# Holding back the loads of q and k of units 6 and 7 behind GpSimd memsets, in an attention and squared-ReLU MLP kernel

## The chip, the cores and the metric

One core of a Trainium2 chip. The metric is device time in microseconds (us) of one execution of the whole program. A "profile" is one execution recorded by the hardware profiler; its span is about 1.8 us shorter than the device time (393.8 against 395.61 us in the kernel before). "Fast" runs are those less than 1.5% above the fastest run of the same kernel; the others carry the label "slow". Engine names in the profile: PE is TensorE (PEld its weight loads), DVE VectorE, ACT ScalarE, POOL GpSimd, SP SyncE; an engine name with a q, such as SPq, is that engine's sequencer, which issues DMAs. L345 is line 345 of the kernel. The granted clock is the share of full speed that TensorE's clock had, 1.00 or 0.50 at any one moment here.

## The reference

```python
# q, k, v: (8, 12, 448, 64) fp32;  w_in: (768, 2048);  w_out: (2048, 768)
scores = q @ k^T / 8
attn   = max(scores, 0)**2 / 448
x      = (attn @ v), heads merged           # (3584, 768)
out    = max(x @ w_in, 0)**2 @ w_out        # (3584, 768) fp32
```

The 96 heads are handled in 24 units of four heads, three units for each of eight batches.

## The kernel before

The kernel is written through its own list scheduler. Every operation is added with a cost; the scheduler simulates five engines, decides an order for each, and then emits the instructions in that order. **The scheduler's times decide only the order.** In the trace a load that the plan starts "not before 50 us" is not held until 50 us by anything: the two planned so here go at 6.18 and 6.66 us (below), just behind the casts that free their buffers (5.03 to 6.16 us).

The load of q or k of a unit into one of four fp32 buffers (`raw`) already has a `gate`, which the kernel before never uses:

```python
    def load_qk(n, w, after=0.0, gate=False):
        b, u = divmod(n, NU)
        buf = Buf("raw")
        ...
        deps = []
        if gate:
            deps.append(plan.add(
                [("POOL", 0.1, 0.1, lambda: nc.gpsimd.memset(buf.tile[0:1, 0, 0:1], 0.0))],
                bufs=[buf], after=after))
        eng, name = (nc.scalar, "ACT") if (n, w) == (0, "q") else (nc.sync, "SP")
        op = plan.add([(name, 0.5, 0.5, lambda: eng.dma_start(out=tile_of(), in_=src), QK)],
                      deps, [buf], after=after)
        return op, buf, tile_of
```

The memset writes one element of the buffer. The load overwrites it, so the program makes the load wait for it: a way to tie a DMA to a place in GpSimd's order.

The start of the kernel, in the order of GpSimd's DMA queue (all of these convert fp32 to fp16 on the way: a load of q or k lands as 224.0 KB on the page, one in fp32 as 448.0 KB):

```python
    for w in "kq":
        raws[0, w] = load_qk(0, w)              # unit 0: SyncE and ScalarE queues, fp32
    ...
    for w in "kq":
        casts[1, w] = load_early(1, w, 1.4, 1.0)   # GpSimd queue
    load_v(0, 1.4, 1.1)
    for w in "kq":
        casts[2, w] = load_early(2, w, 1.4, 1.2)
    load_v(1, 1.4, 1.3)
    load_v(2, 1.4, 1.4)
    w1_ops = [load_w1(0, 1.4, 1.5)]                # w_in, four tiles of 1.6 MB
    w1_ops += [load_w1(i, 8.0, 1.6) for i in range(1, 4)]
    ...                                            # units 3 to 5 and w_out later, same queue
```

Units 6 and up are loaded in fp32 by SyncE, cast on GpSimd (`blk<-raw`, L372) and turned by DMA transposes (`qkt<-blk`, L408). TensorE turns q and k of units 0 to 5 itself (L392). Dummy "filler" matmuls (L932) keep it busy where the plan sees idle time in the first 45 us. L453 are the scores, L518 attn times v, L580 and L629 the product with w_in, L729 and L794 that with w_out.

## Time and profile before

| | |
|---|---|
| median of 3 runs | 393.39 us (391.31 to 393.70) |
| profiled run | 395.61 us, span 393.8 us |
| TensorE busy | 382.4 us (97%) |
| mean granted clock of the profiled run | 0.981 |

First the page of the profile: its first line, and the granted clock in 40 equal slices of the span (about 9.8 us each, in tenths; 9 is 90% or more).

```profile
span 393.8 us, 8375 instructions
...
PEclk9859999999999999999999999999999999999999
```

The third slice has a 5: TensorE ran at about half clock around 20 to 30 us. Next the chain of waits (start, length, what), the work that ended last followed back from the end:

```profile
4.94 10.46 DMA g<-in_q_dram
...
20.40 0.33 PE mm L932
...
26.24 0.41 PE sp L453 x4
...
27.19 2.56 PE mm L629 x6
...
47.17 3.37 PE mm L580 x24
...
70.66 7.97 DMA qkt<-blk
```

In this profile one load, q of unit 2, holds the chain for 10.5 us of the start. The timeline of TensorE (start, length, what, and in brackets the idle time before it and what ended it) shows the gap that it leaves:

```profile
12.23 0.42 PE L518 MATMUL mm<-comb,vs 64*64 64x128 f16 x16
15.44 0.30 PE L392 MATMUL mm<-ident,g 128*64 128x128 f16 x4 [2.79 <-DMA g<-in_q_dram]
```

The timeline of SyncE up to 54 us shows what else was loading:

```profile
0.74 5.82 SPq L345 DMA_DIRECT2D raw<-in_k_dram  x2
6.66 0.42 SPq L345 DMA_DIRECT2D raw<-in_q_dram  x1
52.31 0.37 SPq L345 DMA_DIRECT2D raw<-in_k_dram  x1
53.75 0.37 SPq L345 DMA_DIRECT2D raw<-in_q_dram  x1
```

Two k loads are merged in the first line: unit 0 at 0.74 and unit 6 at 6.18. So both loads of unit 6, 0.92 MB, go out at 6 us, far ahead of their use near 67 us. Those of unit 7 go at 52.31 and 53.75 us, as their buffers hold unit 5 until then: TensorE reads it there until 52.28 and 53.71. GpSimd's timeline has the same late load from another side, since its issue of the last w_in tile had to wait for it; and it has the first casts of unit 6:

```profile
15.68 0.82 POOL L427 DMA_DIRECT2D w<-in_moe_w_in_dram  x1 [3.12 <-DMA g<-in_q_dram]
...
67.22 3.41 POOL L372 CAST blk<-raw 128x896 f16<-128x896 f32 x3
```

Last, busy time by windows of 3.41 us, cut at the moments at which the granted clock changed (the recorded stretches of one clock, but for the last, are 10.24, 13.65 and 361.81 us long in this trace: 3, 4, 106 times 3.41 us; columns: window, its length, PE busy and count, PEld, DVE, ACT, POOL, granted clock, DMA share, GB/s):

```profile
10.07:13.48 3.41, 2.27 (x66) 1.38 (x64) 1.85 (x2) 3.39 (x5) 1.94 (x3) 1.00 1.17 289
13.48:16.89 3.41, 1.45 (x46) 1.03 (x47) 1.05 (x3) 0.68 (x1) 1.19 (x2) 1.00 1.20 230
16.89:20.31 3.42, 3.33 (x53) 1.54 (x48) 2.02 (x4) 3.29 (x4) 2.53 (x4) 0.50 1.24 206
...
27.13:30.54 3.41, 3.41 (x23) 1.22 (x25) 0.72 (x2) 1.41 (x4) 0.00 (x0) 0.50 1.24 207
```

The window with the gap has TensorE busy for 1.45 of 3.41 us; right at its end the clock halves, and it stays at half for four such windows, 13.65 us.

### The profile page before, as it was taken

To read this page: it belongs to the slowest core of one execution; us is meant where nothing else is said; L and a number is where in the kernel's file an instruction comes from. 1 tells how busy PE (TensorE), PEld (TensorE's weight loads), DVE (VectorE), ACT (ScalarE), POOL (GpSimd) and SP (SyncE) were. 2 spreads that over 40 slices of the span, in tenths; PEclk is the share of its full clock that TensorE was granted. 3 is DMA by queue.
4 is the path that set the end of the run, shared out by engine and by line. 5 is a ranking of instruction groups with operands and counts; after the bars stand their busy time and mean duration, and the time that the engine had idled before them with its cause. 6 is when DMAs were issued, how large, how long until landed. Compare 5 with 4: busy or idle time off the path is not lost.

```text
span 393.8 us, 8375 instructions
## 1 busy us (share of the span) xinstructions
PE 382.4 (97%) x3324; PEld 201.6 (51%) x3324; DVE 269.0 (68%) x390; ACT 279.0 (71%) x414; POOL 166.4 (42%) x163
## 2 busy tenths in 40 slices
PE   8699999899999999999999999999999999999995
PEld 4435556454455445544555545544455545555553
DVE  3456878877796687657888665866886767256841
ACT  4758989799867887778977687885886876244111
POOL 7544835477473464354744733522701531001000
PEclk9859999999999999999999999999999999999999
DMA  9999996999837976497177677477383001210243
GB/s 194 244 207 168 147 231 113 195 220 204 165 67 122 240 183 97 134 213 125 54 147 183 158 183 165 84 162 163 60 118 80 2 2 37 65 40 2 50 96 96
DMA packets 69672, 51.34 MB, mean 130 GB/s; under 512 B 36865, under 2 KB 69633, under 8 KB 69633
## 3 DMA queue, kind: packets, MB, share of 16 engines
q1 hardware_dynamic: 52112, 35.86, 37.9%
q0 software_dynamic: 16928, 14.09, 24.5%
q10 hardware_dynamic: 592, 0.85, 0.6%
q8 instruction: 26, 0.43, 0.5%
q14 instruction: 14, 0.11, 0.1%
HBM read 45.61 MB, written 11.01 MB: 144 GB/s over the span
## 4 chain that ended last, share of the span: by engine, by line
PE 89%; DMA 5%; DVE 2%; ACT 2%; POOL 1%; issue 1%; POOLq 0%; DVEq 0%
PE mm L580 37%; PE mm L794 29%; PE sp L453 10%; PE mm L518 8%; DMA g<-in_q_dram 3%; DMA qkt<-blk 2%; PE mm L932 2%; PE mm L629 1%; DVE comb L773 1%; PE mm L729 1%; PE mm L392 1%; POOL g L362 1%; ACT at L487 1%; DVE rel L480 0%; ACT rel L483 0%
## 5 line engine op out<-in xcount | busy, mean ns | idle before, releaser
L580 PE MATMUL mm<-xt,w 128*128 128x448 f16 (+1 forms) x768 | 149.2, 346 | 0.0
L489 POOL TENSOR_TENSOR at<-rel 128x896 f16<-128x896 f32 (+1 forms) x45 | 73.0, 1623 | 115.4 <-ACT rel L483 87.6
L487 ACT ACTIVATE at<-rel 128x896 f16<-128x896 f32 (+1 forms) x123 | 111.9, 932 | 7.1 <-DVE rel L480 4.1
L564 DVE SCALAR_TENSOR_TENSOR g<-mm,g 128x448 f16<-128x448 f32 (+1 forms) x128 | 76.7, 605 | 52.0 <-ACT g L569 51.5
L580 PEld LDWEIGHTS <-w 128*128 128x128 f16 x768 | 72.1, 98 | 70.4 <-issue 12.1
L480 DVE TENSOR_SCALAR rel<-sp 128x896 f32<-128x896 f32 (+2 forms) x87 | 90.1, 1040 | 22.9 <-PE sp L453 21.3
L569 ACT ACTIVATE g<-mm 128x448 f16<-128x448 f32 (+1 forms) x128 | 67.8, 535 | 41.3 <-PE mm L580 40.8
L483 ACT ACTIVATE rel<-sp 128x896 f32<-128x896 f32 (+2 forms) x87 | 78.3, 908 | 9.1 <-PE sp L453 8.4
L794 PEld LDWEIGHTS <-comb 128*128 128x128 f16 x416 | 39.7, 98 | 30.0 <-issue 3.8
L453 PE MATMUL sp<-qkt,qkt 64*64 64x448 f16 (+2 forms) x756 | 52.6, 347 | 2.3 <-DMA qkt<-blk 1.9
L713 ACT ACTIVATE part<-mm 128x384 f32<-128x384 f32 x40 | 19.6, 490 | 40.4 <-PE mm L794 38.8
L372 POOL CAST blk<-raw 128x896 f16<-128x896 f32 x36 | 37.0, 1037 | 24.2 <-issue 12.1
L806 DVE SCALAR_TENSOR_TENSOR part<-mm,part 128x384 f32<-128x384 f32 x52 | 28.6, 554 | 23.6 <-ACT part L713 13.3
L794 PE MATMUL mm<-wt,comb 128*128 128x384 f16 x208 | 36.8, 326 | 0.2 <-DVE comb L773 0.2
L794 PE MATMUL mm<-w,comb 128*128 128x384 f16 x208 | 36.8, 326 | 0.1
L518 PE MATMUL mm<-at,vs 64*64 64x448 f16 (+1 forms) x672 | 35.5, 344 | 0.0
L794 PEld LDWEIGHTS <-g 128*128 128x128 f16 x264 | 25.1, 98 | 19.3 <-issue 3.1
L453 PEld LDWEIGHTS <-qkt 64*64 64x64 f16 x756 | 18.0, 107 | 29.8 <-issue 26.0
L695 POOL COPY rest<-g 128x1024 f16<-128x1024 f16 x8 | 9.8, 1226 | 49.8 <-DVE g L564 49.8
L794 PE MATMUL mm<-w,g 128*128 128x384 f16 x176 | 30.8, 326 | 0.0
L422 POOL DMA_DIRECT2D vs<-in_v_dram x48 | 29.7, 627 | 2.1 <-DMA g<-in_k_dram 0.9
L518 PEld LDWEIGHTS <-vs 64*64 64x64 f16 x756 | 22.7, 111 | 12.5 <-issue 2.9
(60 smaller groups left out, 225.1 us busy)
## 6 DMA issues: line engine op xcount, KB each, us to landing
out_dram<-part SPq DMA_DIRECT2D x108, 96.0 KB, 2.2
raw<-in_k_dram SPq DMA_DIRECT2D x19, 448.0 KB, 3.9
raw<-in_q_dram SPq DMA_DIRECT2D x18, 448.0 KB, 4.5
vs<-in_v_dram POOLq DMA_DIRECT2D x48, 112.0 KB, 4.0
w<-in_moe_w_in_dram POOLq DMA_DIRECT2D x4, 768.0 KB, 16.6
w<-in_moe_w_out_dram POOLq DMA_DIRECT2D x4, 768.0 KB, 13.0
g<-in_k_dram POOLq DMA_DIRECT2D x4, 224.0 KB, 11.5
g<-in_q_dram POOLq DMA_DIRECT2D x4, 224.0 KB, 11.7
```

The source lines that it names most:

```text
L372: return lambda: fn(blk.tile.rearrange("p t (f d) -> p f t d", f=2), tile_of().rearrange("p f (t d) -> p f t d", d=D))
L422: nc.gpsimd.dma_start(out=buf.tile[64 * r:64 * r + 64], in_=src[:, u, hs])
L453: nc.tensor.matmul(sp[64 * c:64 * c + 64, e, c0:c0 + w].rearrange("p (t c) -> p t c", c=TP), lhsT=kT[r, t, 64 * e:64 * e + 64], rhs=qT[r, ...
L480: dve(n, lambda: nc.vector.tensor_scalar(out=rel(), in0=sp.tile[:, :, 0:width], scalar1=0.0, scalar2=SK, op0=ALU.max, op1=ALU.mult)),
L483: act(n, lambda: nc.scalar.activation(out=rel(), in_=sp.tile[:, :, 0:width], func=AF.Relu, scale=SK))],
L487: act(n, lambda: nc.scalar.activation(out=dst(), in_=rel(), func=AF.Square)),
L489: lambda: nc.gpsimd.tensor_mul(dst(), rel(), rel()))],
L518: nc.tensor.matmul(banks[f].tile[64 * e:64 * e + 64, c0:c0 + w], lhsT=vs[r, e ^ c, t * D:(t + 1) * D], rhs=a[r, e, :], start=(t == 0), sto ...
L564: nc.vector.scalar_tensor_tensor(out=dst, in0=src, scalar=0.0, in1=dst, op0=ALU.is_gt, op1=ALU.mult)
L569: nc.scalar.activation(out=dst, in_=src, func=AF.Square)
L580: nc.tensor.matmul(bank.tile[:, c0:c0 + w], lhsT=w1[f // 4][:, m, f % 4 * P:(f % 4 + 1) * P], rhs=xts[b].tile[:, m, cols], start=(m == 0), ...
L794: nc.tensor.matmul(buf.tile[:, 0:HALF], lhsT=lhs()[:, j, :], rhs=w[:, j, :], start=(first and j == 0), stop=(j == NH - 1), skip_group_chec ...
```

## The change

The intent: stop the loads of units 6 and 7 from competing with the start, by using the gate for these two units. The memset is planned at 50 us, so it sits in GpSimd's order after the operations planned before that.

```diff
-                        raws[n, w] = load_qk(n, w, max(50.0, coming(n) - 26.0))
+                        raws[n, w] = load_qk(n, w, max(50.0, coming(n) - 26.0), n < 8)
```

As the scheduler sees the memsets, its order changes too, though not at once: TensorE's order is the same for the first 40% of its instructions.

## The prediction

> **What bounds the kernel now.** TensorE: busy 382.4 of 393.8 us on the page; 89% of the chain of waits. Its direct waits sum to under 7 us (view of waits), so most of what can be won is in the start. There the chain goes through one DMA: the load of q of unit 2, issued at 4.94 us, lands at 15.4, and TensorE idles 2.8 us for it (12.65 to 15.44, timeline). Then the granted clock falls: 1.00 up to 16, 0.50 until about 30 (windows of 2 us). [...]TensorE is recorded busy throughout, so some 6.9 us are lost.
>
> **Why that load is late.** The scheduler's plan starts the loads of unit 6 at 50 us, but the hardware waits only for their buffers, free since the casts of unit 0: issued at 6.1 and 6.7 us (timeline of SyncE). Their 0.92 MB move from about 10 to 15.4 us, while the GpSimd queue (unit 2, v, w_in) moves only 0.66 of some 1.2 MB: 2.6 us lost.[...]
>
> **What the change does.** Four memsets of one element (about 0.1 us each; GpSimd is 42% busy: nothing) stand in GpSimd's order after its third 128x896 square, which ends at 59.6 us before. Loads of unit 6 move from 6 us to behind that; those of unit 7 (52.3 and 53.8 before, against w_out) too. TensorE's order is unchanged over its first 40%; later a few squares and blocks swap: taken as 0 +-1.5 us.
>
> **Gain, at the start.**
> - q of unit 2 lands 2.6 us earlier; TensorE's gap shrinks to under 0.5 us: -2.5 us.
> - Without the gap the clock should stay at 1.0 (chance 75-80%): -6.9 us at most.
> - Not all is kept. Each w_in tile lands about 2.7 us earlier (estimated 19.3, 23.4, 26.6, 30.2), and a full-speed TensorE reaches the second 1.3 us too early. ScalarE must do 17.4 us of work (14 to 40 us) in about 20, and is the chain already at 37 to 43. I give back 3 us.
> Net: about -6.5 us by the mark that was 43 us; everything after it shifts along, bound by TensorE.
>
> **Cost, at 53 to 65 us.** Four loads, 1.84 MB, at some 300 GB/s (seen at 2 to 4 us): 6 to 7 us. The casts began at 67.2 us, 7.6 us after the third square, and DMA was nearly idle from 64 to 68: casts wait under 1 us. The 1.9 us wait for transposes at 77 us stays, shifted.
>
> **Predicted: 387.0 us; 382.5 to 391.5 holds it 8 times in 10.** Faster by over 2%: 0.28; within 2%: 0.70; slower: 0.02.
>
> **What would show it.** Right: no wait of TensorE over 1 us at 11 to 15 us; granted clock 1.0 from 6 to 40; no SyncE load between 7 and 50 us, then four in a row; the first L580 matmul at about 41 us, not 47.1; later stages shifted equally. Wrong: a half-clock stretch anyway (only 2 to 3 us won); TensorE idle before the L629 matmuls, or ScalarE saturated from 20 to 40; casts waiting for DMA at 60 us and a longer transpose wait.
>
> **What would make it wrong.** [...]the throttle's cause isn't the gap; or the later reordering costs or saves over 1.5 us.

2.5 + 6.9 - 3 = 6.4 us, put at about 6.5, and 6.5 below 393.5 is 387.0. The 6.9 us of the clock is the estimate: half of the 13.65 us that the profile before shows at half clock, and that the gap brings the half clock was at this point an inference from one profile, in which the one follows the other. The memsets' 0.1 us was an estimate as well; they were recorded at 88 ns each.

## The result, and the profile after

| | before | changed |
|---|---|---|
| median, runs of this comparison | 393.52 us (391.31 to 393.70, 4 runs) | 387.19 us (387.09 to 387.20, 4 runs) |
| ratio of fast runs | | 0.9851, 95% interval 0.9816 to 0.9886 |
| span of the profiled run | 393.8 us | 385.4 us |
| mean granted clock there | 0.981 | 0.998 |

Ratios in this text are the mean time of one kernel's fast runs over that of the other's of the same rounds, so not quite the ratio of the medians. The change is faster by 1.5%, within 2%.

The page: the 8 and the 5 in the clock row are gone.

```profile
span 385.4 us, 8379 instructions
...
PEclk9999999999999999999999999999999999999999
```

The chain of waits, the lines that answer to those above:

```profile
16.25 0.26 PE sp L453 x4
...
17.55 0.21 PE mm L932
...
20.72 1.29 PE mm L629 x6
...
39.03 3.37 PE mm L580 x24
...
62.53 7.83 DMA qkt<-blk
```

The same six L629 matmuls take 1.29 us in place of 2.56, and the first L580 group starts at 39.03, 8.14 us earlier. TensorE's timeline at the same place:

```profile
11.46 0.42 PE L518 MATMUL mm<-comb,vs 64*64 64x128 f16 x16
11.81 0.30 PE L392 MATMUL mm<-ident,g 128*64 128x128 f16 x4
...
13.99 0.36 PE L518 MATMUL mm<-comb,vs 64*64 64x128 f16 x11
15.16 0.27 PE L518 MATMUL mm<-comb,vs 64*64 64x128 f16 x5 [0.80 <-issue]
```

The turning of q of unit 2 goes at 11.81 without a wait; a smaller gap of 0.80 us appears three us later. The profile names no cause for it ("issue"), but these matmuls read v of unit 2, whose load lands at 14.9 us in this trace. SyncE now issues nothing after unit 0 until 51.5 us (the first line again merges two loads), then four loads in a row:

```profile
0.75 51.14 SPq L345 DMA_DIRECT2D raw<-in_k_dram  x2
52.00 0.41 SPq L345 DMA_DIRECT2D raw<-in_q_dram  x1
52.51 0.41 SPq L345 DMA_DIRECT2D raw<-in_k_dram  x1
53.02 0.42 SPq L345 DMA_DIRECT2D raw<-in_q_dram  x1
```

GpSimd: q of unit 2 has landed by 11.94 in place of 15.68; a w_in tile that releases an issue at 22.90 is the second one; the memsets cost 0.19 us; the casts start without waiting for a load.

```profile
11.94 0.82 POOL L427 DMA_DIRECT2D w<-in_moe_w_in_dram  x1 [0.30 <-DMA g<-in_q_dram]
...
22.90 0.76 POOL L362 DMA_DIRECT2D g<-in_q_dram  x1 [2.38 <-DMA w<-in_moe_w_in_dram]
...
51.40 0.19 POOL L342 MEMSET raw<- 1x1 f32 x4
...
59.09 3.41 POOL L372 CAST blk<-raw 128x896 f16<-128x896 f32 x3
```

The windows, 3.41 us long as before and counted back from the one change of clock in that run, at 383.80 us, and then all that TensorE waited for (view of waits: total us, times, longest):

```profile
8.33:11.75 3.42, 3.42 (x88) 2.38 (x88) 2.37 (x5) 3.41 (x4) 3.07 (x4) 1.00 1.26 202
11.75:15.16 3.41, 2.52 (x92) 1.64 (x80) 3.03 (x5) 3.41 (x5) 3.21 (x4) 1.00 1.26 205
15.16:18.57 3.41, 3.41 (x66) 1.77 (x65) 2.37 (x4) 3.13 (x5) 2.17 (x5) 1.00 1.21 190
```

```profile
PE sp L453 <- DMA qkt<-blk: 1.8, 1, 1.8
PE mm L929 <- DVE part L926: 1.2, 1, 1.2
PE mm L518 <- issue: 0.8, 1, 0.8
```

The emptiest of these windows has 2.52 of 3.41 us, and the clock stays up. What is left is 1.8 us near 70 us, for the DMA transposes of unit 6.

### The profile page after: what moved, and what is told of

It is laid out like the page before. It is cut to its first block, busy times and chain, and to the rows that moved or that the text cites. A ratio compares the mean times of both kernels' runs of the same rounds, so it can differ in the third digit from the quotient of the medians.

```text
span 385.4 us, 8379 instructions
## 1 busy us (share of the span) xinstructions
PE 376.1 (98%) x3324; PEld 200.0 (52%) x3324; DVE 266.2 (69%) x387; ACT 277.1 (72%) x413; POOL 173.1 (45%) x171
## 4 chain that ended last, share of the span: by engine, by line
PE 90%; DMA 4%; DVE 3%; ACT 2%; issue 1%; POOL 0%; POOLq 0%; DVEq 0%
PE mm L580 37%; PE mm L794 29%; PE sp L453 10%; PE mm L518 8%; DMA qkt<-blk 2%; PE mm L932 2%; DMA g<-in_q_dram 2%; DVE comb L773 1%; PE mm L629 1%; PE mm L729 1%; DVE rel L480 1%; PE mm L392 1%; ACT at L487 1%; ACT rel L483 0%; DVE part L806 0%
## 5 line engine op out<-in xcount | busy, mean ns | idle before, releaser
L580 PE MATMUL mm<-xt,w 128*128 128x448 f16 (+1 forms) x768 | 149.0, 346 | 0.0
L489 POOL TENSOR_TENSOR at<-rel 128x896 f16<-128x896 f32 (+1 forms) x49 | 79.9, 1630 | 105.0 <-ACT rel L483 81.0
L487 ACT ACTIVATE at<-rel 128x896 f16<-128x896 f32 (+1 forms) x119 | 108.2, 931 | 3.2 <-PE mm L518 2.3
L580 PEld LDWEIGHTS <-w 128*128 128x128 f16 x768 | 72.1, 98 | 70.6 <-issue 12.3
L480 DVE TENSOR_SCALAR rel<-sp 128x896 f32<-128x896 f32 (+2 forms) x86 | 89.0, 1039 | 18.4 <-PE sp L453 16.6
L483 ACT ACTIVATE rel<-sp 128x896 f32<-128x896 f32 (+2 forms) x88 | 79.2, 908 | 8.0 <-PE sp L453 7.2
L453 PE MATMUL sp<-qkt,qkt 64*64 64x448 f16 (+2 forms) x756 | 51.0, 338 | 2.1 <-DMA qkt<-blk 1.8
L453 PEld LDWEIGHTS <-qkt 64*64 64x64 f16 x756 | 17.7, 105 | 28.0 <-issue 23.8
L518 PEld LDWEIGHTS <-vs 64*64 64x64 f16 x756 | 22.0, 107 | 12.7 <-issue 3.0
## 6 DMA issues: line engine op xcount, KB each, us to landing
g<-in_k_dram POOLq DMA_DIRECT2D x4, 224.0 KB, 11.3
```

Of the source, the lines that this page charges most:

```text
L453: nc.tensor.matmul(sp[64 * c:64 * c + 64, e, c0:c0 + w].rearrange("p (t c) -> p t c", c=TP), lhsT=kT[r, t, 64 * e:64 * e + 64], rhs=qT[r, ...
L480: dve(n, lambda: nc.vector.tensor_scalar(out=rel(), in0=sp.tile[:, :, 0:width], scalar1=0.0, scalar2=SK, op0=ALU.max, op1=ALU.mult)),
L483: act(n, lambda: nc.scalar.activation(out=rel(), in_=sp.tile[:, :, 0:width], func=AF.Relu, scale=SK))],
L487: act(n, lambda: nc.scalar.activation(out=dst(), in_=rel(), func=AF.Square)),
L489: lambda: nc.gpsimd.tensor_mul(dst(), rel(), rel()))],
L518: nc.tensor.matmul(banks[f].tile[64 * e:64 * e + 64, c0:c0 + w], lhsT=vs[r, e ^ c, t * D:(t + 1) * D], rhs=a[r, e, :], start=(t == 0), sto ...
```

## The experiments

The theory: (a) the early loads of unit 6 delay q of unit 2 in the DMA engines; (b) TensorE's gap halves its clock; (c) the half clock is the larger part of the cost. Rivals: the clock falls for another reason; contention of unit 7 with w_out matters; the scheduler's reordering made the gain. Twelve experiments were run, all with correct results. "Clock" below is each run's mean granted clock.

| run | median us (range), runs | clock of the runs | ratio to before in the same rounds |
|---|---|---|---|
| before_again | 392.18 (388.53 to 394.55), 6 | 0.980 to 0.999 | 0.998 (0.991 to 1.005) |
| order_kept | 388.40 (387.82 to 389.69), 6 | 0.993 to 1.0 | 0.991 (0.986 to 0.996) |
| only_unit7 | 391.31 (389.01 to 394.01), 6 | 0.981 to 1.0 | 0.998 (0.992 to 1.004) |
| fill_gap | 389.33 (388.20 to 389.58), 6 | 0.997 to 1.0 | 0.992 (0.987 to 0.997) |
| after_again | 387.70 (387.29 to 389.00), 6 | 0.994 to 1.0 | 0.986 (0.983 to 0.989) |
| gap_back | 392.29 (390.98 to 394.13), 6 | 0.987 to 0.993 | 0.997 (0.994 to 1.001) |
| gap_back_filled | 390.28 (388.96 to 392.36), 6 | 0.996 to 1.0 | 0.992 (0.989 to 0.996) |
| k6_early | 388.14 (387.06 to 389.89), 6 | 0.993 to 1.0 | 0.987 (0.984 to 0.990) |
| gate8 | 385.90 (385.21 to 386.67), 6 | 0.997 to 1.0 | 0.984 (0.980 to 0.988) |
| hold8_14 | 385.85 (385.44 to 389.93), 6 | 0.987 to 1.0 | 0.986 (0.981 to 0.990) |
| after_third | 388.56 (387.15 to 390.10), 6 | 0.993 to 1.0 | 0.990 (0.985 to 0.995) |
| gate8_again | 385.67 (385.35 to 389.26), 6 | 0.990 to 1.0 | 0.983 (0.979 to 0.988) |

The four groups of runs were the first four, the next four, the next two and the last two; each was on another chip.

### before_again: how much the time before hangs on the clock

No edit.

> The kernel before, unchanged, to see its spread run by run with the granted clock of each run. Theory (the time of the kernel before hangs on how many windows of half clock follow the gap): single times differ by steps of about 2 us (391.3, 393.5, 395.6 were seen) and go with the mean granted clock, about 1.7 us of time for each 0.0043 of clock[...]. Rival (the spread is something else, such as DMA): times and clocks unrelated.

Measured: the same program took from 388.5 to 394.6 us in this run, and its clock went from 0.999 to 0.980. With the runs of before there are 48 fast runs (two more, 394.55 and 395.11 us at clock 0.983, are left out; with them the slope below is 281). A straight line through them is 389.3 us + 276 us x (1 - clock), with a correlation of 0.94. Four runs at a clock of at least 0.998 took 389.3 us in the mean; nine at 0.981 or less, 394.4.

It follows that the kernel before is not a 393 us kernel with noise but a 389.3 us kernel that loses 0 to 5 us to half clock, run by run; in the mean 276 x (1 - 0.9882) = 3.3 us. The profiled run, at 395.61 us, was the worst. The expected 1.7 us for each 0.0043 of clock, an estimate that takes half of the time at half clock as lost, came out as 1.2. The estimate would hold if all of TensorE's work took twice as long: the slope would then be the span, 393 us. It is 70% of that. The chains above fit this: the dense L629 group takes 2.56 against 1.29 us, twice as long, but L453 x4 takes 0.41 against 0.26 and L932 0.33 against 0.21, 1.6 times.

Two cautions about the clock figures. The record falls to 0.50 once more at the very end, after TensorE's last matmul (in the changed kernel from 383.80 us on, with TensorE busy for 0.00 us after that), and this alone makes its 0.998. In none of the eight kept profiles at 0.998 to 1.0 was the clock at half during TensorE's work, so amounts worked out from a mean clock are some 0.3 us too large. And each record begins only at 4 to 7 us (6.65 in the first profile, 4.92 in that of the changed kernel); before that the views print 1.00 for want of a record.

The profile of this run (394.55 us) also shows that the first one was unusual. Here q of unit 2 landed at 13.2 us and not at 15.4, and TensorE waited for two loads in turn, q and then v of unit 2. The chain goes through v (first line; then two lines of the view of waits):

```profile
6.32 10.43 DMA vs<-in_v_dram
...
PE mm L392 <- DMA g<-in_q_dram: 1.6, 2, 1.2
PE mm L518 <- DMA vs<-in_v_dram: 1.0, 1, 1.0
```

It is the same in only_unit7 (1.3 and 1.0 us), and in fill_gap too q lands at 13.0 and the chain goes through v. So in three of the four profiles with both loads of unit 6 early, the wait is shared between q and v. Why q was 2 us later in the first profile is not known.

### order_kept: the gain without the reordering

```diff
-        op = plan.add([(name, 0.5, 0.5, lambda: eng.dma_start(out=tile_of(), in_=src), QK)],
+        op = plan.add([(name, 0.5, 0.5, lambda: (n in (6, 7) and nc.gpsimd.memset(tile_of()[0:1, 0, 0:1], 0.0), eng.dma_start(out=tile_of(), in_=src)), QK)],
```

> The kernel before with the same four memsets, emitted together with the loads so that the scheduler does not see them: the order of TensorE, VectorE, ScalarE and SyncE stays as before, only the memsets are added on GpSimd. Theory (all of the gain is the start, the reordering after 40% of TensorE's work is worth nothing): 387 us within 1 us, clock 1.0 throughout, ratio to before about 0.984. Rival (a good part of the gain came from the reordering): over 389 us.

Measured: 388.4 us; ratio 0.991. This is 1.4 us over the expected value, between the theory and its rival, and two of the six runs were at clocks of 0.993 and 0.994, which the theory excluded. The four clean runs took 388.1 us in the mean; those of the changed kernel took 387.4 (below), but on other chips. Its first L580 group starts at 39.03 us as in the changed kernel, so the start is fully there. The profile puts the difference at one place: TensorE waits 2.7 us near 70 us for the transposes of unit 6, against 1.8, and the scores after that wait start 0.93 us later than in the changed kernel (71.42 and 70.49). At the end the two are 1.03 us apart (last VectorE step of the chain at 382.16 and 381.13). So in these two profiles the reordering over the last 310 us is worth about 0.1 us. The edit itself explains the rest only in part: its memsets for unit 7 come one GpSimd operation later, so those loads are issued at 53.75 and 54.23 us in place of 52.51 and 53.02. That this is what makes the transposes later was not tested.

### only_unit7: is the contention with w_out worth anything?

```diff
+        ... the same line, with the memset only for n == 7
```

> The same, but only the two loads of unit 7 are held back; those of unit 6 go at 6 us as before. Theory (only the loads in the start matter): as before, 393.5 us within 1 us, q of unit 2 lands at 15.4, half clock from about 16. Rival (the contention with w_out at 52 to 64 us matters too): faster by 1 us or more, with the start unchanged.

Measured: ratio 0.998, interval 0.992 to 1.004: the same as before. Its median of 391.3 lies 2 us under that of before, which was to be within 1 us, but the clock explains this: its two runs at clock 1.0 took 389.0 and 389.7 us, just what the line of before gives there. The mean of the six, 391.5, is also what the line gives at their mean clock of 0.991 (391.7). So no effect of unit 7 alone was seen. Two expectations missed: q of unit 2 landed at 13.3 us and not at 15.4, and the half clock began at 18.12 us, after the window with the wait for v. In the change unit 7 cannot be seen apart: its loads come after those of unit 6 in SyncE's order anyway.

### fill_gap: early loads as before, but no idle TensorE

Twelve dummy 128x512 matmuls are put into TensorE's order just before the transposes of q of unit 2, in the kernel before; everything else stays.

```diff
-            for t in ts:
+            for t in ["fill"] * 12 * ((n, w, ts[0]) == (2, "q", 0)) + list(ts):
```

The cut leaves out the second changed line, which makes each "fill" a 128x512 matmul of the idle tile into the same PSUM bank. The twelve took 2.76 us in the profile.

> The kernel before, all loads as before, with 12 dummy matmuls (128x512, some 2.6 us) on TensorE just before it waits for q of unit 2. Theory (the idle gap is what halves the clock): the load still lands at about 15.4, but the clock stays at 1.0, and TensorE reaches its first L580 matmul some 4 to 6 us earlier than before; total 388 to 390. Rival 1 (the clock falls for another reason, such as the thin 64x64 matmuls after 16 us): half clock as before and 393 to 394 us. Rival 2 (DMA bound the start anyway, so the clock cost nothing): clock 1.0 but no gain, TensorE idle before the L629 matmuls.

Measured: 389.33 us, clock 0.997 or more in all six runs, range 1.4 us in place of 6. The windows of its profile show the place of the gap filled, and the clock up:

```profile
13.35:16.76 3.41, 3.14 (x72) 1.76 (x70) 1.86 (x4) 1.09 (x3) 2.56 (x3) 1.00 1.21 233
16.76:20.17 3.41, 3.41 (x61) 1.70 (x61) 2.68 (x4) 3.41 (x5) 2.52 (x5) 1.00 1.25 209
```

The first L580 group starts at 41.19 us. So (b) holds: the loads were as before and only TensorE's idle time was filled, and the half clock was gone. One expectation missed: q of unit 2 landed at 13.0 us and not at 15.4, so the dummies, which lasted to 14.5, outlasted the wait for it. The value, 389.3, is also the end of the line above at clock 1. What remains to the changed kernel is about 2 us: TensorE turns q of unit 2 at 14.51 us, after the dummies, in place of 11.81.

### gap_back and gap_back_filled: held loads, with the gap put back

In the changed kernel, one added matmul at the same place reads v of unit 2, whose load lands later, so TensorE idles with no added DMA. The second kernel puts 15 dummies ahead of it (3.41 us in its profile).

```diff
-            for t in ts:
+            for t in ["wait"] * ((n, w, ts[0]) == (2, "q", 0)) + list(ts):
```

Cut as before: the second changed line makes "wait" a matmul that reads v of unit 2. The second kernel has 15 "fill" ahead of it.

> The changed kernel with one added matmul on TensorE just before it turns q of unit 2, which reads v of unit 2 and so waits for that load (it lands at about 14 to 15 us; TensorE is there at 11.8). All loads stay held back, so the gap is back without the DMA contention. Theory (the gap halves the clock): half clock from about 16 us in most runs; time 389 us plus up to 6, spread by several us from run to run, going with the clock. Rival (the contention, not the gap, cost the time): clock 1.0 and 389 to 390 us at most.

> The same added wait for v of unit 2, with 15 dummy matmuls of 128x512 (some 3.2 us) ahead of it, so that TensorE is as late as in the run with the gap, but not idle. Theory: clock 1.0, spread under 1 us, 389.5 us within 1 us. Rival (the delay itself costs, not the clock): same time and same clock as with the gap.

Measured: with the gap 392.29 us, and the clock at 0.987 to 0.993 in every run; filled 390.28 us and a clock of 0.996 or more. TensorE idles 3.63 us in the profile of the first, and its windows show the clock fall at the end of the empty one, with all loads of units 6 and 7 still held:

```profile
10.72:14.13 3.41, 0.85 (x29) 0.47 (x23) 1.10 (x2) 2.74 (x3) 3.07 (x4) 1.00 1.25 203
14.13:17.55 3.42, 2.35 (x35) 1.32 (x39) 1.17 (x3) 0.01 (x1) 1.02 (x2) 0.50 1.18 189
```

The filled kernel turns q of unit 2 as late (15.89 us) as the one with the gap (15.72). In the latter's profile one of the three windows at half clock lies near 75 us (75.57 to 78.99), after a wait of 2.3 us for the transposes of unit 6, so the gap in the start answers for two thirds of the clock that was lost there.

Together with fill_gap this is a two by two: early or held loads, idle or filled gap. The clock follows the idleness in both rows and not the loads. The filled one spread over 3.4 us, more than the 1 us expected; one run of 392.36 us at clock 0.996 stays unexplained.

### k6_early: half of the early bytes

The edit of order_kept, with the memset for q of unit 6 and for unit 7, but not for k of unit 6.

> The kernel before in its own order, memsets hidden from the scheduler, with q of unit 6 and both loads of unit 7 held back but k of unit 6 let go at 6 us: half of the early bytes (0.46 MB). Theory (bytes ahead of q of unit 2 set the gap): q of unit 2 lands about 1.3 us later than with all held, a gap of about 1 us; clock mostly 1.0, about 389 us, a run or two slower. Rival (any load there is enough): as before, 392 to 394 us with the clock down in most runs.

Measured: 388.14 us, about as fast as with all held (388.40). TensorE waits 1.08 us for q of unit 2, and its window keeps the clock:

```profile
10.75:14.16 3.41, 2.33 (x77) 1.62 (x74) 2.08 (x4) 2.77 (x3) 1.91 (x3) 1.00 1.21 244
```

So (a) holds: q of unit 2 lands at 11.3 to 12.1 us in the nine profiles with no early load, at 12.7 with 0.46 MB, and with 0.92 MB at 13.0 to 13.3 in three profiles and at 15.4 in the first. In the profile of k6_early the clock was at half for one window after the wait for the transposes near 70 us (72.19 to 75.60). The clock can fall there too, and did in before_again (76.36 to 79.77) and gap_back; so a part of the clock lost by before is lost there and not in the start.

### after_again and after_third: is the changed kernel immune?

No edit.

> The changed kernel once more, for its spread with the granted clock of each run (only four runs of it are known, 387.1 to 387.2). Theory (its start has no gap long enough to halve the clock[...]): all runs within 0.5 us of 387.2, clock 0.997 or above. Rival[...]: one run in four or so at 389 to 391 us with a clock near 0.990.

> The changed kernel, on the same chip and in the same rounds as the version that holds the loads of unit 8 too, as the two had been timed on different chips. Theory (the wait near 70 us costs it 1.8 us, and now and then one window of half clock after it): 387.3 us, one or two runs of six 1.3 to 1.7 us slower at a clock near 0.994.

Measured: the theory of the first, that all runs are at clock 0.997 or more, fails. Of the 16 runs of the changed kernel, twelve have such a clock and took 387.4 us in the mean; four took 389.0 to 390.1 us with clocks of 0.993 to 0.996. The first four runs had been lucky. The second expected one or two slow runs of six, 1.3 to 1.7 us slower; three came, 2.1 to 2.7 us above the clean ones. No profiles were kept of the four, so it is not shown whether the clock fell in the start or near 70 us.

### gate8 and hold8_14: the wait near 70 us

In the changed kernel the loads of unit 8 are issued at 60.04 and 61.95 us, between the transposes of unit 6 (60.51 and 62.53). Two ways to move them:

```diff
 gate8, from the changed kernel
-   load_qk(n, w, max(50.0, coming(n) - 26.0), n < 8)
+   load_qk(n, w, max(50.0, coming(n) - 26.0), n < 9)
 hold8_14, from the changed kernel
+   load_qk(n, w, max(50.0, coming(n) - (14.0 if n == 8 else 26.0)), n < 8)
```

> The changed kernel with the loads of unit 8 held by memsets as well, which the scheduler places behind the first three casts; on SyncE these loads then come behind the transposes of unit 6. Theory (the 1.8 to 2.2 us that TensorE waits near 70 us for the transposes of unit 6 come from the loads of k and q of unit 8, which are issued at 60.0 and 62.0 us and share the DMA engines with the transposes issued at 60.5 to 64.8): that wait falls under 0.7 us, the time to about 385.7 us, and no window of half clock follows near 72 us. Rival (the transposes are late because the casts on GpSimd are, and take their time by themselves): wait and time as in the changed kernel, 387.5 us.

> The changed kernel with the loads of unit 8 not gated but planned 12 us later, so that on SyncE they come behind four transposes and the first stores. Theory: as in the run with the gate, wait near 70 us under 0.7 us and about 385.7 us, unless the cast of unit 8 then waits for its load. Rival: 387.5 us; if the loads come too late, a wait for the transposes of unit 8 near 85 us and up to 1 us more.

Measured: 385.90 and 385.85 us, as expected. The wait for transposes is no longer among TensorE's waits in either profile. SyncE's timeline of gate8 shows three transposes together, and the loads of unit 8 behind them:

```profile
60.28 4.17 SPq L408 DMA_TRANSPOSE qkt<-blk  x3
64.50 1.23 SPq L675 DMA_DIRECT2D out_dram<-part  x2
65.83 0.54 SPq L345 DMA_DIRECT2D raw<-in_k_dram  x1
```

Both edits also move other instructions, so the 1.5 us are shown for the version, and for the loads of unit 8 as its cause only as far as two different edits agree. One run of hold8_14 took 389.93 us at clock 0.987, and its profile caught it. TensorE's gap in the start was only 1.06 us there, yet the clock fell to 0.50 after the window with it, in which TensorE was busy for 2.27 us:

```profile
13.11:16.53 3.42, 2.27 (x65) 1.20 (x53) 1.96 (x4) 3.42 (x5) 2.46 (x3) 1.00 1.20 191
16.53:19.94 3.41, 3.41 (x41) 1.35 (x45) 2.33 (x4) 2.00 (x3) 2.54 (x4) 0.50 1.23 205
```

Up to 16 us TensorE's order there is the changed kernel's, so the change leaves a small risk of the half clock.

### gate8_again: beside the changed kernel on one chip

No edit to gate8.

> The version with the loads of unit 8 held too, beside the changed kernel on one chip. Theory: 385.7 us, 1.6 us below the changed kernel in the same rounds, ratio between them 0.996, every run at a clock of 0.997 or more. Rival (the 385.9 us came from the other chip): within 0.5 us of the changed kernel.

Measured: means of 386.2 us against 388.6 us of after_third in the same rounds, a ratio of 0.994; medians 385.67 and 388.56. One run of six took 389.26 us at clock 0.990, so "every run at 0.997 or more" missed; of the twelve runs of this version eleven are at 385.2 to 386.7. Its twelve runs average 386.1 us, the changed kernel's sixteen 388.0. It is the fastest beside hold8_14, from which it can't be told apart.

## Why the prediction was right or wrong

The time, 387.0 predicted and 387.19 measured in the comparison, was right. The mechanism was right: early loads, gap, half clock. Two terms of the sum were mis-sized; they offset each other in part, and that the number still fits to 0.2 us is luck (below).

- **The early loads of unit 6 delay q of unit 2**: right, shown by k6_early and by the timeline. By the packets of the first profile the GpSimd queue moves 0.20 MB in each us from 8 to 10 us, and 0.08 to 0.10 from 10 to 14 us, while 0.18 to 0.20 go over SyncE's queue; in the changed kernel it keeps 0.20 over that time. From 10 to 15.4 us of the first profile it moves 0.56 MB, where the prediction had 0.66. That the chain goes through q of unit 2 alone holds for the profiled run; in the others v of unit 2 is delayed as well (before_again).
- **The gap, "-2.5 us"**: right for the profiled pair. TensorE resumed 3.63 us earlier and lost 0.80 of it in the new gap, so -2.8. As a lasting gain it is less: the clean runs of before and changed kernel differ by 389.3 - 387.4 = 1.9 us.
- **The clock, "-6.9 us at most"**: mis-sized. It took half of the 13.65 us at half clock. Of the 8.14 us by which the first L580 group moved, 2.8 are the gap; the 5.3 left are, by difference, the clock's. (By the slope of before_again such a stretch costs 276 / 393 of the half, about 4.8 us.) In the chains the thin matmuls take 1.6 times as long at half clock (L453 x4 0.41 against 0.26 us) and not twice. And the profiled run was a bad one; in the mean the half clock costs before 3.3 us and the changed kernel 276 x (1 - 0.9978) = 0.6 us.
- **"I give back 3 us"**: wrong; nothing was given back. The first L580 group came at 39.03 us and not at about 41, and its shift of 8.14 us is no less than gap and clock together (2.8 + 4.8 by the slope). The reason given for it did not come: TensorE does not wait for w_in (no such line in the view of waits). The second tile had landed by 22.90, near the estimate of 23.4, and TensorE reached it only at 23.36. About half of the 3 us offset the clock term, which was 1.6 us too large.
- **The luck**: the net gain was put at 6.5 us and was 8.1 on the profiled run. 387.0 is 6.5 below 393.5, about the median of before, not below the 395.61 of the run on which the gain was worked out; 8.1 below that is 387.5. The gain too small and the lower starting point cancelled, and the four runs of the changed kernel were all clean ones.
- **"Everything after it shifts along"**: right; 8.14 us at 39.03, 8.28 at the wait for transposes (78.77 to 70.49), 8.4 at the end.
- **The cost at 53 to 65 us, casts waiting under 1 us, memsets nothing**: right; the casts begin 8.13 us earlier with no wait for a load, the memsets take 0.19 us. The wait near 70 us stayed at 1.8.
- **Reordering 0 +- 1.5 us**: right; about 0.1 us after 71 us, by order_kept.
- **"The clock should stay at 1.0 (chance 75-80%)"**: so it did in twelve of sixteen runs.
- The size over all runs is smaller than in the comparison: 16 runs of the changed kernel average 388.0 us and 48 fast runs of before 392.5, a gain of 4.6 us, or 1.2%. Of this 2.7 us are clock (276 x (0.9978 - 0.9882)) and 1.9 us are the rest, so (c) holds in the mean, though not by much.

What stays open: why q of unit 2 landed 2 us later in the first profile than in the three others with the same early loads, and what decides whether the clock falls and for how long. With those same early loads it fell at 16.89, 14.92 and 18.12 us in three profiles. TensorE's recorded busy time in one window does not decide it: in the start the clock was at half after windows busy for 1.45 (before), 2.18 (only_unit7) and 2.27 us (hold8_14), and still at full after windows of 2.15 (only_unit7) and 2.33 us (k6_early). Nor does it decide how long: near 70 us in k6_early the half clock lasted one window, busy for 3.41 us, and in the start of before four, busy for 3.33 to 3.41 us each.

## What to carry to other kernels

A plan's start time held nothing on the chip here: the loads went as soon as their buffers and their queue were free (6.18 and 6.66 us for a planned 50). So look in the trace for loads issued long before their use, and tie such a load to an instruction that really runs at that time. When a kernel's time spreads by some per cent, plot time against granted clock before explaining anything; one profile then says which run you caught, not what the kernel costs, and a second profile of the same kernel may show another wait. TensorE's gap of 2.79 us cost more here by the half clock after it than by itself (5.3 and 2.8 us in the profiled pair), and in hold8_14 a gap of 1.06 us had half clock after it too. Filling the gap with dummy matmuls shows in one experiment which of the two you have (fill_gap: clock 0.997 or more in all six runs).
